# Sliding-window attention and a two-layer MLP in one kernel: the first batch's v by heads, w_in's parts moved forward in the queues, and another split of the last output block

## The chip, the cores and the metric

The kernel runs on one core of a Trainium2 chip. A core has five engines, each with its own in-order queue of instructions: TensorE (PE in the profile; its weight loads are listed apart as PEld), VectorE (DVE), ScalarE (ACT), GpSimd (POOL) and SyncE (SP). DMAs are issued from the queues of SP, ACT and POOL and are carried by sixteen DMA engines that all queues share. The metric is the device time of one execution in microseconds (us), lower is better; the median of three runs before the change is 323.84 us (323.29 to 324.63).

## The reference

Attention over 8 batches, 8 heads, 576 positions and a head size of 64, with a distance bias per head and a causal window of 128; its output, as 4608 tokens of 512 features, goes through two matrices with a hard-swish between them. Inputs and output are float32.

```python
scores = scale * np.matmul(q, k.transpose(0, 1, 3, 2))
bias = slopes[:, None, None] * (-np.abs(rel))[None, :, :]
mask = (rel >= 0) & (rel < window)              # window = 128
scores = np.where(mask, scores + bias[None], -1000000000.0)
attn = softmax(scores)                           # with 1e-09 added to the sum
x = np.matmul(attn, v)                           # -> (4608, 512)
h = x @ w_in                                     # w_in: 512 x 2048
out = (h * np.clip(h + 3.0, 0.0, 6.0) / 6.0) @ w_out   # w_out: 2048 x 512
```

## The kernel before

**Units of work.** Attention goes by pairs of heads: pair g = 4 b + hp is heads 2 hp and 2 hp + 1 of batch b, so there are 32 pairs. A pair's 576 positions are five blocks of 128 (the last half filled). Because of the window, a block of queries sees its own block of keys (the "diagonal", tile scd, lines 285 to 297) and the one before (the "off-diagonal", tile sco, lines 313 to 329). For a pair the steps are: q and k are cast to bf16 (tile pr) and transposed on TensorE (tile tp, line 219 in batch 0, lines 242 and 254 later; from batch 4 on by DMA through tbuf, line 199); the transposed pieces are copied from PSUM to qTb and kTb; scores; exponential on ACT to pd and po; masks on POOL (lines 354, 364, 370); the product with v (tile wide or av, lines 383 and 391), where a column of ones in vbuf gives the sum; on DVE a reciprocal and a product (lines 401 and 402, 412 and 413) to avs; then `back` (line 421) transposes avs to xT, the MLP's input.

In batch 0 the bias and the mask are added on TensorE, by matmuls of the identity with a table (tables_diag, line 266, and tables_off, line 299), which the exponential then takes in one instruction of 1024 columns a tile (lines 348 and 335). From batch 1 on the diagonal goes without a table: `exp_diag` makes two exponentials of 512 columns with a bias (line 351), each followed by a mask on POOL (line 354).

The MLP goes by nine blocks nt of 512 tokens. Of each, sixteen "ups" (moe_up, line 462: four matmuls of 512 columns at line 451, a Relu on ACT at line 470, and a product on DVE at line 471 into gbuf) and sixteen "downs" (moe_down, line 474: four matmuls at line 483; every fourth ends an output block of 128 rows, which is copied to osb and stored).

**Order.** The program's order is written out by hand, and each engine runs its instructions in that order. Attention of one batch is interleaved with the MLP of tokens that are ready: `fill(n)` (line 511) issues the next n units, ups and downs in the order of the strings ORDER (line 501). `first_batch` (line 546) is pairs 0 to 3 and the loading of batch 1; `second_batch` (line 606) is pairs 4 to 7, the first block's ups and the loading of w_out and batch 2; `segment` (line 657) is all the rest.

**Loads.** q and k of batch 0 come as eight runs of 288 KB (load_run, line 90), from SP's and ACT's queues. v of batch 0 comes from SP as five blocks of 128 positions, each for all heads (load_tokens, line 108), in packets of 256 B. q and k of batches 1 and 2 come by load_double (line 96): for four heads (a half dp of the batch) and one of q and k, two DMAs of 288 KB. w_in comes in four parts of 512 columns (load_w_in, line 165) and w_out in four of 512 rows (load_w_out, line 170), cast to bf16 on the way, all from POOL's queue; part i of w_in is first needed by up 4 i. Until w_out arrives, its room holds pd and po of batch 0, and the room of gbuf[1] holds those of batch 1. A one-element memset on POOL (lines 176 and 626) is used to hold back a load into a buffer: the load writes the same element and so waits for POOL to come to it.

**PSUM.** Eight banks: two wide buffers "sc" for scores (and for `wide`), two "h", one "av" and one "o".

The last output block (block 8, rows 384 to 511) is made in lines 485 to 493: after the sixteenth matmul of 512 columns ACT copies columns 0 to 255 and DVE 256 to 511 of the same PSUM tile, and ACT's and SP's queues store one half each.

## Time and profile before

| | |
|---|---|
| median of 3 runs | 323.84 us (323.29 to 324.63) |
| the profiled execution's own time | 324.27 us |
| its span, first to last instruction | 322.6 us |
| granted TensorE clock, mean | 0.999 |
| DMA packets, bytes | 131425, 51.90 MB, 118976 of them under 512 B |
| first transpose of batch 0 starts | 5.56 us |
| values of pair 3 start | 19.95 us |
| first up matmul starts | 21.12 us |
| scores of pair 4 start | 26.05 us |
| values of pair 4 start | 41.33 us |
| first down starts | 51.72 us |
| values of pair 8 start | 64.05 us |
| last matmuls end | 318.8 us |

All later times are from the start of the span of this one profiled execution. A row of the timeline shows start, duration, engine, line, operation, what it writes and reads, and in brackets how long the engine was idle before it and whose work or DMA ended that wait. A row of the table by stretches shows the stretch, its length, then each engine's busy time with the number of instructions, the granted clock, the mean busy share of the sixteen DMA engines (packets overlap, so it can exceed 1) and GB/s. Where a text gives the time at which a DMA landed, it is that of the semaphore update in the same trace.

Landings before the change that the steps use: v's blocks of batch 0 at 10.60, 11.76, 13.95, 15.43 and 16.07; w_in's parts, issued at 12.37, 17.82, 27.21 and 27.94, at 20.34, 27.67, 34.33 and 37.73; v of batch 1, last block, at 38.70; w_out's parts, issued at 40.83 to 43.06, at 47.95, 51.65, 54.68 and 58.13; v of batch 2, fourth and fifth block, at 62.56 and 63.53.

### The profile page before, as it was taken

How to read it: one execution, taken by the hardware profiler on the slowest of the kernel's cores; microseconds unless marked ns; L12 is line 12 of the kernel's file. 1: busy time of each engine (PE TensorE's matmuls, PEld its weight loads, DVE VectorE, ACT ScalarE, POOL GpSimd, SP SyncE). 2: the span in 40 equal slices, each digit the busy share in tenths (PEclk: the TensorE clock that was granted, in tenths of full speed). 3: DMA queues.
4: the chain of work that ended last, by engine and by line, in shares of the span. 5: the costliest groups of instructions: out<-in, count | busy, mean ns of one | idle time of the engine just before them, and what ended most of it. 6: DMA issues, size and time to landing. Idle time of an engine off the chain costs nothing.

```text
span 322.6 us, 7017 instructions
## 1 busy us (share of the span) xinstructions
PE 311.8 (97%) x2722; PEld 166.1 (52%) x2722; DVE 173.1 (54%) x338; ACT 195.2 (61%) x334; POOL 140.1 (43%) x249
## 2 busy tenths in 40 slices
PE   7889999999999999999999999999999999999995
PEld 6565465554554454555677654455444444444442
DVE  6767574554356555555555555555556455455500
ACT  4749976877777666766676667666764344244301
POOL 7465592693593767356745665463331000000000
PEclk9999999999999999999999999999999999999999
DMA  7999999999999999999999999932112100000111
GB/s 279 223 323 201 273 243 201 231 232 200 202 255 177 219 214 184 200 223 205 187 191 200 225 190 199 220 84 79 26 50 84 56 34 35 33 33 33 67 65 65
DMA packets 131425, 51.90 MB, mean 161 GB/s; under 512 B 118976, under 2 KB 123328, under 8 KB 131392
## 3 DMA queue, kind: packets, MB, share of 16 engines
q1 hardware_dynamic: 126160, 45.43, 65.7%
q0 software_dynamic: 4224, 4.19, 8.2%
q10 hardware_dynamic: 1008, 1.84, 1.5%
q8 instruction: 21, 0.34, 0.4%
q14 instruction: 12, 0.10, 0.1%
HBM read 36.70 MB, written 9.44 MB: 143 GB/s over the span
## 4 chain that ended last, share of the span: by engine, by line
PE 82%; DMA 7%; ACT 4%; DVE 2%; POOL 2%; issue 1%; POOLq 0%
PE ops L483 37%; PE hps L451 33%; DMA ldbuf<-in_q_dram 3%; PE scd L296 3%; DMA qTb<-tbuf 2%; DMA w_in_sb<-in_moe_w_in_dram 2%; PE av L391 2%; PE av L383 2%; ACT r L470 2%; PE sco L328 1%; PE w L153 1%; ACT kTb L244 1%; DVE kTb L220 1%; PE tp L219 1%; POOL tbuf L194 1%
## 5 line engine op out<-in xcount | busy, mean ns | idle before, releaser
L471 DVE SCALAR_TENSOR_TENSOR gbuf<-r,hps 128x512 bf16<-128x512 f32 x144 | 98.7, 687 | 103.1 <-ACT r L470 101.6
L470 ACT ACTIVATE r<-hps,bias 128x512 f32<-128x512 f32 x144 | 99.0, 689 | 90.1 <-PE hps L451 89.7
L451 PE MATMUL hps<-xT,w_in_sb 128*128 128x512 bf16 (+1 forms) x640 | 144.9, 358 | 1.3 <-DMA w_in_sb<-in_moe_w_in_dram 0.4
L483 PE MATMUL ops<-w_out_sb,gbuf 128*128 128x512 bf16 x576 | 141.3, 379 | 0.0
L451 PEld LDWEIGHTS <-w_in_sb 128*128 128x128 bf16 x640 | 58.9, 98 | 54.7 <-DMA w_in_sb<-in_moe_w_in_dram 1.4
L483 PEld LDWEIGHTS <-gbuf 128*128 128x128 bf16 x576 | 53.8, 98 | 59.1
L354 POOL TENSOR_SCALAR_AFFINE_SELECT pd<-pd 128x512 bf16<-128x512 bf16 x48 | 29.5, 631 | 34.6 <-ACT pd L351 34.6
L364 POOL TENSOR_SCALAR_AFFINE_SELECT po<-po 128x512 bf16<-128x512 bf16 x48 | 30.1, 632 | 32.2 <-ACT po L361 32.1
L351 ACT ACTIVATE pd<-scd,bias_d 128x512 bf16<-128x512 f32 x48 | 31.5, 684 | 5.0 <-PE scd L296 3.6
L194 POOL CAST tbuf<-ldbuf 128x512 bf16<-128x512 f32 (+1 forms) x45 | 25.5, 611 | 18.7 <-DMA qTb<-tbuf 10.4
L498 DVE COPY osb<-ops 128x512 f32<-128x512 f32 x33 | 22.7, 687 | 20.3 <-PE ops L483 20.3
L361 ACT ACTIVATE po<-sco,bias_o 128x512 bf16<-128x512 f32 x48 | 33.0, 688 | 0.0
L402 DVE TENSOR_TENSOR avs<-av,rc 128x384 bf16<-128x384 f32 (+1 forms) x48 | 23.6, 491 | 1.6
L391 PEld LDWEIGHTS <-pd 128*128 128x128 bf16 x192 | 14.4, 97 | 8.3 <-POOL tbuf L194 0.5
L383 PE MATMUL av<-vbuf,po 128*128 128x65 bf16 x192 | 18.1, 193 | 0.5 <-POOL po L364 0.5
L391 PE MATMUL av<-vbuf,pd 128*128 128x65 bf16 x192 | 17.6, 194 | 0.3 <-ACT kTb L244 0.3
L187 POOL CAST vbuf<-ldbuf 128x1024 bf16<-128x1024 f32 x14 | 14.3, 1041 | 4.5 <-DMA ldbuf<-in_v_dram 4.5
L383 PEld LDWEIGHTS <-po 128*128 128x128 bf16 x192 | 14.4, 98 | 3.7 <-POOL po L364 0.7
L367 ACT ACTIVATE p4buf<-sco,bias_d 128x64 bf16<-128x64 f32 x48 | 15.5, 323 | 0.0
L227 POOL CAST pr<-ldbuf 128x576 bf16<-128x576 f32 x20 | 12.8, 667 | 4.1 <-DMA ldbuf<-in_q_dram 2.1
L296 PE MATMUL scd<-qTb,kTb 64*128 64x128 bf16 x256 | 12.7, 219 | 1.7 <-DVE kTb L220 0.9
L296 PEld LDWEIGHTS <-kTb 64*128 64x128 bf16 x256 | 7.2, 94 | 13.4 <-issue 9.7
(94 smaller groups left out, 208.9 us busy)
## 6 DMA issues: line engine op xcount, KB each, us to landing
out_dram<-osb SPq DMA_DIRECT2D x33, 256.0 KB, 2.4
ldbuf<-in_v_dram SPq DMA_DIRECT2D x32, 256.0 KB, 5.5
ldbuf<-in_q_dram SPq DMA_DIRECT2D x20, 256.0 KB, 4.8
ldbuf<-in_k_dram SPq DMA_DIRECT2D x16, 256.0 KB, 4.6
ldbuf<-in_q_dram SPq DMA_DIRECT2D x12, 288.0 KB, 7.2
ldbuf<-in_k_dram SPq DMA_DIRECT2D x12, 288.0 KB, 7.0
w_in_sb<-in_moe_w_in_dram POOLq DMA_DIRECT2D x4, 512.0 KB, 8.9
w_out_sb<-in_moe_w_out_dram POOLq DMA_DIRECT2D x4, 512.0 KB, 11.2
```

The costliest lines, as they stand in the source:

```text
L194: nc.gpsimd.tensor_copy(out=tbuf[:m, :, j, :], in_=s[:m, j, :, :].rearrange("p (i e) d -> p i (e d)", e=2))
L296: nc.tensor.matmul(scd[:, e, ts(j, 128)], lhsT=kT[r, j, :], rhs=qT[r, j, :], start=first, stop=first or j == 3)
L351: nc.scalar.activation(out=pd[:, e, :, :].rearrange("p j c -> p (j c)"), in_=sc[:, e, :], func=ACT.Exp, bias=bias_d[:, h:h + 1], scale=scale)
L354: nc.gpsimd.affine_select(out=pd[:, e, :, :], in_=pd[:, e, :, :], pattern=[[0, 4], [1, 128]], channel_multiplier=-1, base=0, compare_op=AL ...
L361: nc.scalar.activation(out=po[:, e, :, :].rearrange("p j c -> p (j c)"), in_=sc[:, e, :], func=ACT.Exp, bias=bias_o[:, h:h + 1], scale=scale)
L364: nc.gpsimd.affine_select(out=po[:, e, :, :], in_=po[:, e, :, :], pattern=[[0, 4], [-1, 128]], channel_multiplier=1, base=-1, compare_op=A ...
L383: nc.tensor.matmul(out_av, lhsT=po[:, e, qt % 4, :], rhs=vb[:, qt - 1, h, :], start=True, stop=False)
L391: nc.tensor.matmul(out_av, lhsT=d, rhs=vb[:, qt, h, :], start=(qt == 0), stop=True)
L451: nc.tensor.matmul(hps[:, lo:hi], lhsT=w_in_sb[:, ks, ts(ms, 128)], rhs=xT[:, ks, ds(src, hi - lo)], start=(ks == 0), stop=(ks == n_ks - 1))
L470: nc.scalar.activation(out=r6, in_=hps, func=ACT.Relu, bias=bias3[:, 0:1], scale=1.0 / 6.0)
L471: nc.vector.scalar_tensor_tensor(out=gts[nt][:, ms, :], in0=r6, scalar=1.0, in1=hps, op0=ALU.min, op1=ALU.mult)
L483: nc.tensor.matmul(ops[nt, sub], lhsT=gts[nt][:, ms, ts(sub, 128)], rhs=w_out_sb[:, ms, :], start=(ms == 0), stop=(ms == n_ms - 1))
```

## The change

Three things are changed, and the order around them.

1. v of batch 0 is loaded by heads: first the half-filled last block for all heads, then eight loads, each the four full blocks of one head (128 KB, packets of 256 B as before). It is cast by pairs of heads, all on POOL. The values of pairs 0 and 1 are computed between the scores of later pairs, each head in a PSUM bank of its own (`attend_split`). Transposes of q and of k are separate calls with a bank each and are issued a pair earlier; the casts of pairs 2 and 3 go ahead. Ten warm-up matmuls ahead of the first transposes become eight behind them. Pair 3's diagonal goes without a table, as in later batches.
2. On POOL, load_w_in(0) goes ahead of six of the eight heads' casts, load_w_in(1) is issued with two memsets that hold back the loads of batch 1's second half, load_w_in(2) goes ahead of the casts of that half, load_w_in(3) in the midst of them, and a memset behind it holds back v of batch 1. w_out's parts 0 and 1 go behind a k cast of batch 2, parts 2 and 3 behind pair 7's masks and the q cast. The string of block 1's units and the fills in second_batch are arranged anew.
3. The last output block is computed as 384 and 128 columns in two banks: sixteen matmuls and ACT's copy and store for the first, then sixteen, DVE's copy and SP's store for the second.

```diff
+    def load_heads(b):
+        t = tokens(b, "v")
+        nc.sync.dma_start(out=t[:LAST, 4, :, :],
+                          in_=v[b, :, ds(512, LAST), :].rearrange("h p d -> p h d"))
+        for h in range(H):
+            nc.sync.dma_start(out=t[:, 0:4, h, :],
+                              in_=v[b, h, 0:512, :].rearrange("(j p) d -> p j d", p=128))
...
     def second_w_in():
-        nc.gpsimd.memset(w_out_sb[:, 4, 0:1], 0.0)
+        for i in range(2):
+            nc.gpsimd.memset(ldbuf[i][:, 2 * RT * D:2 * RT * D + 1], 0.0)
         load_w_in(1)
...
     def diag_tabled(g):
-        return g < NP
+        return g < NP - 1
...
+    def attend_split(g, tags):
+        avs = st[g, "avs"] = small.tile([128, NQ, 2, D], BF16, tag="avs", name="avs")
+        for e, tag in enumerate(tags):
+            av = BANKS[tag].tile([128, NQ, W], FP32, tag=tag, name="ave",
+                                 padded_shape=[128, NQ, 102])
+            av_matmuls(g, range(NQ), lambda qt, e: av[:, qt, :], (e,))
+            rc = small.tile([128, NQ, 1], FP32, tag="rcs", name="rcs")
+            nc.vector.reciprocal(rc, av[:, :, D:W])
+            nc.vector.tensor_tensor(out=avs[:, :, e, :], in0=av[:, :, 0:D],
+                                    in1=rc.to_broadcast([128, NQ, D]), op=ALU.mult)
...
+    def last_rows(nt, sub, cut=384):
+        rows = ds(nt * NT + sub * 128, 128)
+        osb = opool.tile([128, d_model], FP32, tag="osb", name="osb")
+        for lo, hi, tag, copy, eng in ((0, cut, "o", nc.scalar.copy, nc.scalar),
+                                       (cut, d_model, "h", nc.vector.tensor_copy, nc.sync)):
+            ps = BANKS[tag].tile([128, hi - lo], FP32, tag=tag, name="ops",
+                                 padded_shape=[128, d_model])
+            for ms in range(n_ms):
+                nc.tensor.matmul(ps, lhsT=gts[nt][:, ms, ts(sub, 128)],
+                                 rhs=w_out_sb[:, ms, lo:hi],
+                                 start=(ms == 0), stop=(ms == n_ms - 1))
+            copy(out=osb[:, lo:hi], in_=ps)
+            eng.dma_start(out=out[rows, lo:hi], in_=osb[:, lo:hi])
...
-    ORDER = [("UUDUDUUDUD", "UUDUDUDUD", "UDUDUDD", "UUDDDD"),
+    ORDER = [("UUDUUDUUDUUD", "UDUDUDUD", "UDUDUDD", "UDDDD"),
...
     def first_batch():
-        prepare(0, (V, A))
+        prepare(0, "qk", (V, A))
         warm_up(20)
         tables_diag(0)
         tables_off(0)
-        warm_up(10)
-        transposes(0, (V, A))
+        transposes(0, "q", "h", V)
+        transposes(0, "k", "h", A)
+        prepare(1, "qk", (P, V))
+        warm_up(8)
         scores_diag(0)
-        prepare(1, (P, V))
-        transposes(1, (V, V))
+        transposes(1, "q", "o", V)
+        transposes(1, "k", "av", V)
         scores_off(0)
         exp_full(0)
+        prepare(2, "qk", (P, V))
+        prepare(3, "qk", (P, V))
+        cast_tail(0, P)
+        cast_pair(0, 0, P)
+        load_w_in(0)
+        for hp in range(1, NP):
+            cast_pair(0, hp, P)
+        for nm in "kq":
+            load_double(1, 0, nm, nc.sync)
         scores_diag(1)
...
+        attend_split(0, ("h", "h"))
         scores_off(2)
-        exp_full(2)
+        exp_off_full(2)
         scores_diag(3)
+        exp_diag(3, 0)
+        exp_diag(3, 1)
+        attend_split(1, ("av", "h"))
+        tables_off(3)
         scores_off(3)
-        exp_full(3)
-        cast_v(0, 0, V)
-        cast_v(0, 1, P)
-        load_w_in(0)
-        cast_v(0, 2, V)
-        cast_v(0, 3, V)
-        cast_v(0, 4, P)
-        for dp in range(2):
-            for nm in "kq":
-                load_double(1, dp, nm, nc.sync)
-        load_tokens(1, "v")
-        attend(0)
-        attend(1)
+        exp_off_full(3)
         back(0)
         attend(2)
         back(1)
+        attend(3)
         prepare_double(1, 0, (P, P), early=second_w_in)
-        attend(3)
+        for nm in "kq":
+            load_double(1, 1, nm, nc.sync)
         back(2)
         up_begin(0, 0, 3)
         back(3)
-        wide_double(1, 0, "q", V)
-        prepare_double(1, 1, (P, P))
         load_w_in(2)
+        prepare_double(1, 1, (P,), "k")
         load_w_in(3)
+        nc.gpsimd.memset(ldbuf[3][:, 0:1], 0.0)
+        prepare_double(1, 1, (P,), "q")
+        tokens(1, "v")
+        load_tokens(1, "v")
         for dp in range(2):
             for nm in "kq":
                 load_double(2, dp, nm, nc.sync)
         up_begin(0, 1, 3)
         done[0] = NP
         fill(1)
-        wide_double(1, 0, "k", A)
+        wide_double(1, 0, "k", V)
         fill(2)
+        wide_double(1, 0, "q", A)
+        fill(1)
...
+        prepare_double(2, 0, (P,), "k")
-        for i in range(4):
+        for i in range(2):
             load_w_out(i)
...
-        prepare_double(2, 0, (P, P))
+        prepare_double(2, 0, (P,), "q")
+        load_w_out(2)
+        load_w_out(3)
         nc.gpsimd.memset(ldbuf[2][:, 0:1], 0.0)
         load_tokens(2, "v")
...
-        fill(1)
-        attend(NP)
+        attend_split(NP, ("av", "o"))
```

The second batch's fills, and the place of its transposes of the second half: the fills of pairs 4, 5 and 6 were 2 and 1, 2 and 1, 1 and 2; they become 1 and 2, 2 and 2, 1 and 1. The wide transposes of k and q of the second half stood ahead of the scores of pairs 4 and 5; they now stand ahead of and behind those of pair 5.

## Prediction

> **What bounds the kernel now.** I read the page first, then TensorE's rows in order of time, then the DMA share by stretches, last the rows at the end. The page (engine sums, then 40 slices):
>
> ```profile
> PE 311.8 (97%) x2722; PEld 166.1 (52%) x2722; DVE 173.1 (54%) x338; ACT 195.2 (61%) x334; POOL 140.1 (43%) x249
> PEclk9999999999999999999999999999999999999999
> DMA  7999999999999999999999999932112100000111
> ```
>
> TensorE (PE) is busy for 97%, its granted clock is full, and nothing here takes work off it but two table matmuls. So only its 10.8 us without work can be won: the rows of idle time in front of an instruction sum to 7.0 us, and 3.8 us follow its last matmul. The DMA row is the second bound: saturated from the second slice to the 25th. These rows of TensorE (start, duration, and in brackets the idle time before it and its releaser) hold most of what can go:
>
> ```profile
> 7.05 0.40 PE L296 MATMUL scd<-qTb,kTb 64*128 64x128 bf16 x8 [0.74 <-ACT kTb L220]
> 9.37 0.40 PE L296 MATMUL scd<-qTb,kTb 64*128 64x128 bf16 x8 [0.21 <-DVE kTb L220]
> 12.23 0.40 PE L296 MATMUL scd<-qTb,kTb 64*128 64x128 bf16 x8 [0.37 <-DVE kTb L220]
> 15.10 0.40 PE L296 MATMUL scd<-qTb,kTb 64*128 64x128 bf16 x8 [0.37 <-DVE kTb L220]
> 22.01 0.38 PE L451 MATMUL hps<-xT,w_in_sb 128*128 128x512 bf16 x1 [0.29 <-ACT xT L438]
> 27.72 1.04 PE L451 MATMUL hps<-xT,w_in_sb 128*128 128x512 bf16 x4 [0.31 <-DVE gbuf L471]
> 34.38 1.04 PE L451 MATMUL hps<-xT,w_in_sb 128*128 128x512 bf16 x4 [0.45 <-DMA w_in_sb<-in_moe_w_in_dram]
> ```
>
> Two are DMA waits: 34.38 by name, and 27.72, where w_in's part 1 lands at 27.67, the moment at which DVE's row ends too. Then batch 2, where TensorE shows no wait but has little slack. POOL's cast of v (first row) waits for its DMA and ends at 63.74; TensorE multiplies by it from 64.05:
>
> ```profile
> 62.70 1.04 POOL L187 CAST vbuf<-ldbuf 128x1024 bf16<-128x1024 f32 x1 [0.74 <-DMA ldbuf<-in_v_dram]
> 64.05 0.23 PE L391 MATMUL av<-vbuf,pd 128*128 128x65 bf16 x2
> ```
>
> That slack of 0.3 us decides most of this forecast: whoever moves TensorE ahead by more meets that v.
>
> **Step 1, batch 0 up to pair 3's values: 2.0 us earlier.** (a) Ten warm-ups lie at 4.91 to 5.56 ahead of the first transposes, though DVE's cast of q ends at 5.19. They go behind the transposes, as eight, into the 0.74 us gap: the transposes begin at 5.22, 0.34 us earlier. (b) DVE and TensorE wait for each other here (DVE's copies at 10.75 and 13.62 follow 1.44 and 0.88 us of idleness). With transposes issued a pair ahead into banks "o" and "av", DVE runs on: from 6.4, casts of k 1 to 3 at 0.65 to 0.74 us and copies of pairs 1 to 3 at a pitch of 0.68 us (7.89 to 8.57), six of them, with a short wait for k 3's landing at 9.67: the last copy ends at 13.2, before at 15.0. v's three DVE casts (0.42 us each) move to POOL at 0.61 us. (c) ACT then paces: exponentials of 1.02 us, pair 3's diagonal as two of 0.63 us in place of one of 1.02 (+0.24), the last ending at 17.0 where it was 17.5. Two table matmuls of 512 columns go (0.43 us of TensorE); POOL gets two masks of 0.62 us, in its queue behind v's casts and ahead of batch 1's. (d) attend_split does 18 value matmuls as two nines between the scores; its halves have no row. A half holds 5 reciprocals and 320 products; two of them cost at least the whole (0.22 + 0.82 us, rows of L412 and L413) and at most twice that. I take 1.3 us; they lie on DVE, free after 13.2, beside ACT's work. Then follow back(0), attend(2), back(1), paced by ACT's copies (0.64 us) and TensorE's transposes. Sum: pair 3's values begin at 17.9, before at 19.95.
>
> **Step 2, w_in part 0.** Its first use would move from 21.12 to 18.9, but it lands at 20.34. POOL issues it after q 3's cast, v's last block and heads 0 and 1: at 12.0, before at 12.37. No row shows a load of one head (512 packets of 256 B). Nearest are v's blocks: one of 256 KB lands 1.2 to 2.2 us after the one ahead of it, the last, of 128 KB, 0.64 us after. So I cost nine loads like five, and part 0 lands at 19.9; if undisturbed at 19.0, if heads 0 and 1 come late at 20.8. The DMA page of the Trainium skill ("DMA: Bandwidth & Descriptors", Bandwidth) speaks against small transfers: batch to 1 MiB or more. By it nine loads lose against five; the 0.64 us above says that half the bytes took half the time while the queue was full.
>
> **Step 3, parts 1 to 3.** Part 1 follows the first k cast of batch 1, which now stands on POOL behind pair 3's masks: issued at 18.65, before at 17.82. But the loads of batch 1's second half (four of 288 KB, 0.75 us each at landing intervals) wait for the two memsets issued with it, where before all eight were ahead of it. Both sets, 3.0 us and about 3.3 us (the step between landings of w_out's parts is 3.0 to 3.7), run side by side after 21: I take 26.5 for part 1, ends 25 and 28. Its first user, up 4, is ready at 25.9, so it starts at 26.5 instead of 27.72, with 0.6 us of transposes (L254) left for later: gain 0.6. Parts 2 and 3 are issued at about 22 and 26.5 rather than both at 27.21; part 2 would land near 31, before 34.33, so the 0.45 us stall goes. Pair 4's values, at 41.33 before, would start near 40; the gain is then 1.1 to 1.5 us. What is late next is batch 1's v, now behind part 3: cast at 39.7 before, and the same set of transfers stands ahead of it. That fits by 0.3 us.
>
> **Step 4, the wall at batch 2.** All that is loaded before batch 2's v is the same set in both kernels, and DMA runs without a break from 2 us to 58 us. So v of batch 2 comes earlier only by what DMA wastes now. The DMA share by stretches (the last two columns are share and GB/s):
>
> ```profile
> 12.00:14.00 2.00, 1.77 (x57) 1.35 (x58) 1.12 (x3) 1.42 (x2) 1.25 (x2) 1.00 1.16 179
> 14.00:16.00 2.00, 1.63 (x24) 0.69 (x20) 2.00 (x5) 1.49 (x2) 0.00 (x0) 1.00 0.99 224
> 26.00:28.00 2.00, 1.69 (x17) 0.70 (x15) 1.61 (x3) 2.00 (x5) 1.41 (x3) 1.00 1.09 233
> 28.00:30.00 2.00, 2.00 (x21) 1.06 (x20) 2.00 (x3) 1.78 (x4) 1.92 (x3) 1.00 0.93 172
> 58.00:60.00 2.00, 2.00 (x11) 0.90 (x10) 1.13 (x2) 2.00 (x6) 0.78 (x2) 1.00 0.66 146
> 60.00:62.00 2.00, 2.00 (x29) 1.06 (x27) 1.54 (x3) 1.56 (x4) 1.86 (x3) 1.00 0.86 231
> ```
>
> Stretches with 256 B packets reach 1.2. Against that the first four lack 0.63 x 2 us / 1.2 = 1.05 us, the last two 1.5 us. The change touches the first four: v's half-filled last block goes first, under the k and q loads, and batch 1's v no longer runs alone at 27 to 30. It leaves the bubble at 58 to 62, where SP issues v's fourth block only at 58.2. A new hole of about 0.3 us opens near 21. So v of batch 2 comes 0.75 us earlier; ends 2.3 us earlier (all waste gone) and 1.5 us later (no waste gone, and the later issues below cost DMA time). Gain kept at 64 us: 0.3 + 0.7 = 1.0 us.
>
> w_out is the cover here: parts 0 and 1 go behind two k casts of batch 2, parts 2 and 3 behind pair 7's masks, issued at about 46.2 instead of 42.33. Part 3 landed at 58.13 for a use at 58.57. The new order puts two more ups (0.87 us each) ahead of that use, so it stays near 58.5 with TensorE 1.5 us ahead: cost nothing, with 0.2 us to spare. After 64 us TensorE has only short waits (the longest 0.35 us at 108) and SP's issues follow its pace, so what is kept there is kept.
>
> **Step 5, the end: 0.55 us.** ACT and DVE copy one half each, one after the other, and SP issues last:
>
> ```profile
> 318.85 0.37 ACT L489 COPY osb<-ops 128x256 f32<-128x256 f32 x1 [2.87 <-PE ops L483]
> 319.25 0.42 DVE L490 COPY osb<-ops 128x256 f32<-128x256 f32 x1 [6.62 <-ACT osb L489]
> 319.70 0.33 SPq L492 DMA_DIRECT2D out_dram<-osb  x1
> ```
>
> Now the first 384 columns are complete while the sixteen 128-column matmuls (0.055 us each, the pace of the ten warm-ups, 0.88 us) still run; ACT's copy (between 0.37 and 0.58, say 0.48) hides under them, and DVE copies 128 columns in 0.29 us (by the slope from 0.42 for 256 to 0.69 for 512). SP issues 0.34 us after the last matmul, before 0.88. Bounds: 0.2 (the two copies still serialize) and 0.7 (the smaller store lands sooner too). The additional weight loads cost nothing by the 65-column value matmuls, each with its own 128x128 weights, at a pitch of 0.03 us (16.67, 16.70, 16.73). The Trainium skill, "TensorE: Matmul & The Clock Gate", Back-to-back issue gap, speaks against it: it gives about 81 ns for each 128-column matmul with its weight load. As an estimate from that page the part would take 1.3 us and the end would win only 0.1 us.
>
> **Sum.** 1.0 + 0.55 = 1.55 us off the profiled execution's 324.27 us (span 322.6) is 322.7. The median of the runs is 0.43 us below the profiled one, so on its scale 323.84 - 1.55 = 322.3 us.
>
> **Rivals.** (A) The front's gain passes whole: part 1 in time for 25.9 and v of batch 2 with 1.5 us or more to spare. Then 1.85 us at pair 4's values (39.5 against 41.33) and more with the bubble at 58 gone: 2.4 to 3.2 us, about 321.2. For it: 2.5 us of DMA waste exist. Against: half of them at a place that the change doesn't touch. (B) Nothing but the end: v of batch 2 as late as now gives 0.3 + 0.55, parts of w_in late again less: 323.2. For it: the same bytes stand ahead. (C) Slower: POOL's queue becomes a chain. Batch 1's v waits for a memset behind part 3, which waits for two k casts, which wait for loads that wait for a memset behind another cast; then k of batch 2, then w_out, then v of batch 2. Every us that this chain comes late reaches 64.05. It decides from 0.85 us (0.3 + 0.55); at 3 us late, 66.7 at that place, the time is 323.84 + 3.0 - 0.85 = 326.0. For it: each link is a real wait; against: DMA has other work at each of them.
>
> **Chances.** Forecast 0.38 (gain 0.9 to 2.3), A 0.29, B 0.16, C 0.17. 0.5%, about what a measurement of this kernel can tell from no change, is 1.6 us: the forecast falls 0.22 beyond and 0.16 within it, A beyond, B within, C 0.14 slower and 0.03 within. Faster 0.51, same 0.35, slower 0.14. From 320.6 (nearly all of A) to 325.4 (C up to 2.4 us late) 8 in 10 should lie.
>
> **What would show it.** Pair 3's values near 18 us and the first up matmul held by w_in until 19.9 (steps 1 and 2); up 4 near 26.5 with a wait for w_in (3); batch 2's first value matmul waiting for POOL's cast of v, near 63 (4): without that wait A, with it at 64 or later B or C; SP's last issue 0.34 us behind the last matmul (5). It is wrong from the root if DMA's order, not its total, sets when v of batch 2 lands.

## The result and the profile after

The kernel after takes 327.66 us (median of 6 runs, 327.48 to 328.93), the one before 324.08 us on the same chip (6 runs, 323.29 to 325.86): ratio 1.0101, 95% interval 1.0080 to 1.0122. It is slower, by more than the prediction's range allowed. The profiled execution took 327.62 us, its span is 325.9. The page's lines that answer to those of before:

```profile
PE 313.1 (96%) x2734; PEld 167.9 (52%) x2734; DVE 173.3 (53%) x342; ACT 195.5 (60%) x335; POOL 142.5 (44%) x255
...
PEclk9999999999999999999999999999999999999999
DMA  7989999999999999999899999942011200000111
```

The DMA row has 8s where it had 9s. TensorE's busy time grew by 1.3 us and its idle time by 2.0 us. Of the 1.3 us, 0.7 lie between 4.5 and 7.5 us (3.00 us busy against 2.26) and are no added work: in this execution the full clock was granted from 7.46 us on, in that of before from 4.56, and 36 transposes took 1.17 us at 5.38 but 0.75 us at 7.77. That late start costs nothing further on: the run e10 below, with the full clock from 4.24 on, comes to the first row here at the same 13.70. TensorE's rows in order of time:

```profile
13.70 0.38 PE L308 MATMUL scd<-qTb,kTb 64*128 64x128 bf16 x7 [0.59 <-issue]
...
19.22 0.44 PE L455 MATMUL tb<-ident,avs 128*128 128x128 bf16 x5 [0.72 <-ACT xT L461]
19.49 0.23 PE L403 MATMUL wide<-vbuf,w_out_sb 128*128 128x65 bf16 x2
...
28.68 0.39 PE L474 MATMUL hps<-xT,w_in_sb 128*128 128x512 bf16 x1 [1.32 <-DMA w_in_sb<-in_moe_w_in_dram]
...
66.80 0.23 PE L403 MATMUL av<-vbuf,pd 128*128 128x65 bf16 x2
...
67.67 0.19 PE L403 MATMUL av<-vbuf,pd 128*128 128x65 bf16 x1 [0.49 <-POOL vbuf L199]
```

The row of before that answers to the last one:

```profile
64.27 0.19 PE L391 MATMUL av<-vbuf,pd 128*128 128x65 bf16 x1
```

Pair 3's values start at 19.49 (before 19.95), the first up at 20.85 (21.12): batch 0 is a little earlier. Up 4 (28.68, before 27.72) waits 1.32 us for w_in's part 1; pair 4's values start at 42.90 (41.33). Batch 2's first value matmuls start at 66.80 (64.05). The eighth of them is the first to read v's second cast; it now waits for POOL until 67.67, where before it started at 64.27 without a wait: 3.40 us late. The last matmul ends 3.72 us later (322.53 against 318.81). So nearly all of the loss is there by batch 2.

Where it starts, in POOL's rows. First before, then after:

```profile
16.76 0.67 POOL L227 CAST pr<-ldbuf 128x576 bf16<-128x576 f32 x1
17.78 0.10 POOL L176 MEMSET w_out_sb<- 128x1 bf16 x1 [0.35 <-PE wide L391]
17.82 0.74 POOL L166 DMA_DIRECT2D w_in_sb<-in_moe_w_in_dram  x1
```

```profile
17.49 0.63 POOL L192 CAST vbuf<-ldbuf 128x512 bf16<-128x512 f32 x1 [2.15 <-DMA ldbuf<-in_v_dram]
18.07 1.22 POOL L366 TENSOR_SCALAR_AFFINE_SELECT w_out_sb<-w_out_sb 128x512 bf16<-128x512 bf16 x2
20.71 0.66 POOL L241 CAST pr<-ldbuf 128x576 bf16<-128x576 f32 x1 [1.42 <-DMA ldbuf<-in_k_dram]
21.31 0.14 POOL L185 MEMSET ldbuf<- 128x1 f32 x2
21.39 0.76 POOL L174 DMA_DIRECT2D w_in_sb<-in_moe_w_in_dram  x1
```

POOL first waits 2.15 us for head 7, the last of v's loads (landed 17.44), so that pair 3's masks end at 19.29. Then the first cast of batch 1's k waits 1.42 us for its own load, which landed at 20.56 (before 16.61). Behind the cast stand the memsets that hold the second half's loads, and w_in's part 1: issued 3.6 us later than before. What that does to the DMA engines shows in the stretches (granted clock, DMA share and GB/s are the last three columns), first before, then after:

```profile
16.00:24.00 8.00, 6.64 (x122) 5.31 (x122) 5.02 (x11) 3.76 (x6) 5.15 (x9) 1.00 1.11 323
24.00:40.00 16.00, 15.25 (x147) 7.88 (x144) 10.49 (x14) 15.02 (x23) 8.32 (x13) 1.00 1.13 233
40.00:64.00 24.00, 23.33 (x248) 13.43 (x247) 14.80 (x26) 18.60 (x31) 15.01 (x25) 1.00 1.08 225
```

```profile
16.00:24.00 8.00, 6.38 (x100) 4.39 (x97) 3.88 (x10) 5.18 (x9) 5.09 (x11) 1.00 0.85 213
24.00:40.00 16.00, 14.27 (x136) 7.60 (x133) 11.22 (x14) 13.67 (x21) 7.58 (x13) 1.00 1.18 240
40.00:64.00 24.00, 22.00 (x231) 12.28 (x225) 13.51 (x25) 18.47 (x30) 14.63 (x25) 1.00 1.07 228
```

From 16 to 24 us the DMA engines deliver (323 - 213) x 8 us = 0.88 MB less. Later they win back (240 - 233) x 16 + (228 - 225) x 24 = 0.18 MB. The missing 0.70 MB at 228 GB/s are 3.1 us. Another 0.33 MB were missing at 16 us already (3.74 against 4.07 MB), which makes 4.5 us in all; the fourth block of batch 2's v lands 3.9 us later (66.45 against 62.56). The hole itself, and the four stretches in which the prediction wanted waste to go:

```profile
12.00:14.00 2.00, 1.41 (x36) 0.70 (x30) 1.59 (x3) 0.79 (x1) 1.61 (x3) 1.00 0.87 163
14.00:16.00 2.00, 2.00 (x54) 1.71 (x52) 1.00 (x4) 1.48 (x2) 0.99 (x2) 1.00 0.99 136
20.00:22.00 2.00, 1.51 (x16) 0.72 (x13) 1.04 (x2) 0.97 (x2) 1.29 (x4) 1.00 0.58 213
22.00:24.00 2.00, 1.83 (x20) 1.19 (x19) 0.32 (x1) 0.74 (x2) 2.00 (x5) 1.00 0.57 54
26.00:28.00 2.00, 0.94 (x11) 0.36 (x9) 1.78 (x4) 1.91 (x3) 0.67 (x1) 1.00 1.15 292
28.00:30.00 2.00, 1.32 (x8) 0.66 (x8) 0.40 (x1) 1.08 (x3) 0.98 (x2) 1.00 1.14 298
```

At 12 to 16 less is moved than before (163 and 136 GB/s against 179 and 224), 26 to 30 is better (292 and 298 against 233 and 172), and 20 to 24 is new. The end, last: ACT's copy no longer ends the kernel, and SP issues 0.36 us behind the last matmul (0.89 before).

```profile
321.68 0.48 ACT L508 COPY osb<-ops 128x384 f32<-128x384 f32 x1 [2.01 <-PE ops L505]
...
322.57 0.29 DVE L508 COPY osb<-ops 128x128 f32<-128x128 f32 x1 [6.25 <-PE ops L505]
322.89 0.33 SPq L509 DMA_DIRECT2D out_dram<-osb  x1
```

### The profile page after: what moved, and what is told of

Same layout as the page of the kernel before. It is cut to its first block, busy times and chain, and to the rows that moved or that the text cites. A ratio compares the mean times of both kernels' runs of the same rounds, so it can differ in the third digit from the quotient of the medians.

```text
span 325.9 us, 7055 instructions
## 1 busy us (share of the span) xinstructions
PE 313.1 (96%) x2734; PEld 167.9 (52%) x2734; DVE 173.3 (53%) x342; ACT 195.5 (60%) x335; POOL 142.5 (44%) x255
## 4 chain that ended last, share of the span: by engine, by line
PE 80%; DMA 6%; POOL 4%; SPq 4%; issue 2%; ACT 1%; DVE 1%; POOLq 0%
PE ops L524 36%; PE hps L474 31%; DMA ldbuf<-in_v_dram 4%; SPq L112 4%; PE scd L308 2%; PE av L403 2%; DMA ldbuf<-in_k_dram 2%; PE av L395 2%; PE sco L340 1%; PE ops L505 1%; PE w L161 1%; POOL pr L241 1%; PE tp L232 1%; ACT xT L461 1%; POOL vbuf L199 1%
## 5 line engine op out<-in xcount | busy, mean ns | idle before, releaser
L524 PE MATMUL ops<-w_out_sb,gbuf 128*128 128x512 bf16 x560 | 138.0, 379 | 0.4 <-DMA w_out_sb<-in_moe_w_out_dram 0.3
L524 PEld LDWEIGHTS <-gbuf 128*128 128x128 bf16 x560 | 52.1, 98 | 57.7 <-issue 0.6
L403 PE MATMUL av<-vbuf,pd 128*128 128x65 bf16 x192 | 17.9, 194 | 0.8 <-POOL vbuf L199 0.5
```

The source lines that it names most:

```text
L403: nc.tensor.matmul(out_av, lhsT=d, rhs=vb[:, qt, h, :], start=(qt == 0), stop=True)
L524: nc.tensor.matmul(ops[nt, sub], lhsT=gts[nt][:, ms, ts(sub, 128)], rhs=w_out_sb[:, ms, :], start=(ms == 0), stop=(ms == n_ms - 1))
```

## The experiments

The theory at first (T): the holds leave the DMA engines without work at 20 to 24, and all later loads are late by it. Rivals: batch 0's new order costs by itself; w_out's new place costs (W). Medians and ratios stand against the kernel before on the same chip (324.25 to 324.83 us). Before moved by up to 0.75 us between chips, so small differences between kernels on different chips are read from the ratios. A profile is one execution and can lie 1 to 3 us from the median.

The granted clock has to be read beside the times. In all executions of the change, e1, e2, e3 and e9 its mean was 0.998 or more. In other kernels some executions had less (0.988 to 0.995 in e10 and e11), and most of these are 1 to 3 us longer than the rest of the same kernel; where the argument needs it, the text says so.

**The end alone** (e1_tail_only): the kernel before with `last_rows`.

> The kernel before with the last output block as 384 and 128 columns and nothing else. In the changed kernel 3.36 us lie between the end of the last matmul and the end of the span, before 3.8. Theory T (the loss is all in the loading chain of the first 65 us): this part alone gives 0.3 to 0.6 us less than before, about 323.5. Rival (the split of the last block costs as much as it wins, as two groups of matmuls, two banks): within 0.2 us of before, or slower.

323.69 us, ratio 0.9979 (0.9959 to 0.9999): 0.77 us faster. The end's gain is real, though the interval only just leaves out no change, and what precedes it in the change loses 3.58 + 0.77 = 4.35 us by the medians, 4.0 by the ratios.

**Without the first hold** (e2_no_hold): all eight loads of batch 1's k and q ahead of POOL's cast.

```diff
-        for i in range(2):
-            nc.gpsimd.memset(ldbuf[i][:, 2 * RT * D:2 * RT * D + 1], 0.0)
...
-        for nm in "kq":
-            load_double(1, 0, nm, nc.sync)
+        for dp in range(2):
+            for nm in "kq":
+                load_double(1, dp, nm, nc.sync)
```

> The changed kernel, in which the second half of batch 1's q and k is issued right behind the first half and no memset holds it back; w_in's part 1 still follows the first k cast. Theory T (the two memsets behind a cast that waits for k's landing at 20.6 stop SP's queue, DMA runs dry at 21 to 23, and all that follows comes late by that): the hole closes, v of batch 2 lands 1.5 to 2.5 us earlier than 66.45, the time is 325.0 to 326.2, and the wait for w_in part 1 (1.3 us) may stay or grow, since these loads then stand ahead of it. Rival R (loading v by heads is what costs): no change, 327.4 or more.

325.01 us, 1.0026 (1.0007 to 1.0045): 2.65 us of the loss gone by the medians (2.4 by the ratios), as T said. In all ten executions the clock was 0.998 or more. 16 to 24 us delivers as much as before or more, and v of batch 2 no longer holds TensorE:

```profile
16.00:24.00 8.00, 6.40 (x94) 4.35 (x90) 3.71 (x11) 5.30 (x10) 5.67 (x9) 1.00 1.10 350
```

**w_in's part 1 ahead of the cast** (e3_w1_early, the memsets with it), and **both** (e5_both).

```diff
-        prepare_double(1, 0, (P, P), early=second_w_in)
+        second_w_in()
+        prepare_double(1, 0, (P, P))
```

> The changed kernel, in which the two memsets and w_in's part 1 go ahead of the first k cast of batch 1 on POOL instead of behind it, so that they no longer wait for k's landing: issued at 19.4 instead of 21.4. Theory T: all links of the chain come 1.5 to 2 us earlier, the wait for part 1 (1.3 us) goes, pair 8's values start near 65.5 instead of 67.7; time 325.3 to 326.2. Rival R: no change but the wait for part 1, whose 1.3 us come back as a wait for v of batch 2: 327.4.

> The changed kernel without the hold on the second half of batch 1's q and k, and with w_in's part 1 ahead of the first k cast on POOL (the edits of the two runs before together). Theory T (one chain, cut at two places): part 1 lands before 27, its wait goes, and DMA has no hole near 21; the time is 324.0 to 325.0, no better than the sum of the two gains allows, since v of batch 2 lands at about 62.5 to 63 by DMA's total. If the two edits were about different losses, their gains (2.6 and 1.9 us) would add up to 323.2.

e3: 325.79 us, 1.0048 (1.0033 to 1.0063), as T said, again with 0.998 or more in all ten. e5: 325.77 us, 1.0037 (1.0014 to 1.0060). The two edits don't add up, and T's 324 to 325 for e5 is missed by 0.8: with all loads early, part 1 stands among the second half's loads and lands at 28.5, with a wait of 1.16 us.

**v by blocks of positions** (e4_v_blocks): `load_heads(0)` replaced by `load_tokens(0, "v")`.

> The changed kernel with v of batch 0 loaded in five blocks for all heads as before, and cast by pairs of heads as in the change (each cast then needs all five blocks, so pairs 0 and 1 come later). Rival R (nine loads by head are what costs, the last lands at 17.44 where the last block landed at 16.07, and k of batch 1 is issued 1.2 us later): 1 us or more faster, 326.5 or less. Theory T: the start of the chain (k's landing at 20.6) moves by at most 1 us, w_in's part 0 is issued 3 to 4 us later as it stands behind the casts of pair 0; the time gets longer, 327.7 to 330.

328.64 us, 1.0133 (1.0110 to 1.0156): loading v as before does not bring the time back. It does not clear the loading by heads either. Against T, k's landing moved by 3.8 us, to 16.77 (k was issued at 12.25, with part 0 behind it at 17.40), so how v is loaded does bear on when k lands. What e4 loses, it loses elsewhere: all four executions had a clock of 0.989 to 0.995, and pair 0's values need all blocks and wait:

```profile
17.51 0.19 PE L403 MATMUL ave<-vbuf,w_out_sb 128*128 128x65 bf16 x1 [3.18 <-POOL vbuf L192]
```

**The holds on the kernel before** (e6_hold_on_before): the memsets, the second half and v of batch 1 behind the first k cast.

> The kernel before with the hold alone: two memsets behind the first k cast, together with w_in's part 1 as in the change; the loads of batch 1's second half and its v follow behind them on SP. Theory T (the hold costs by what it waits for): before, k lands at 16.6 and the cast ends at 17.4, so the loads are issued at 17.6 while DMA still has work until 21.5: within 0.6 us of before, 323.5 to 324.8. Rival H (holding these loads back costs as such, since fewer transfers are queued): 1.5 us or more slower than before, as in the changed kernel, 325.5 to 326.5.

325.57 us, 1.0038 (1.0012 to 1.0063): by the time inside H's interval, but only 1.1 us slower than before on the same chip, where H asked for 1.5 or more. The holds cost there too, but less where k lands early (17.41 in its profile).

**w_out's place** (e7_w_out_back: e5 with w_out's loads, batch 2's casts and ORDER of before; e12_no_w_out_23: the change without the loads of w_out's rows 1024 to 2047, so their products are not the reference's).

> As e5_both, and in addition w_out's four parts and batch 2's casts at their places of before, with the old string of block 1's units. Theory T (w_out and v of batch 2 stand in one queue that the front has already made late, and the two casts ahead of w_out wait for loads that have landed by then): within 0.6 us of e5_both. Rival W (the part of the loss that e2 left, 1 us against before, is w_out behind the casts): 0.7 us or more faster than e5_both.

> The changed kernel that leaves out the loads of w_out's parts 2 and 3 (rows 1024 to 2047; what then stands in their room is used instead): 6.6 us less for DMA ahead of batch 2's v, and nothing else changed. Theory T (what makes batch 2 late is that v lands behind all other transfers): pair 8's values no longer wait; D 3 neither; of the 3.6 us by which the first values of pair 8 are late against before, 1.5 to 2.5 go, and the time is 325.2 to 326.2. Rival (all of the lateness is made before 53 us, where the first down stands 1.6 us late, and by TensorE's own waits): 327 or more.

e7: 324.97 us, 1.0017 (0.9995 to 1.0038), 0.8 us less than e5: slightly for W. e12: 325.08 us, 1.0023 (0.9994 to 1.0053), 2.6 us less than the change. Without those two loads v of batch 2 lands in time, and pair 8's values start at 65.87 with no wait: the wall at batch 2 carries most of the loss to the end.

**Pair 3's transposes later** (e8_swap3: e5 with them behind pair 2's diagonal scores).

> As e5_both, with pair 3's transposes behind pair 2's diagonal scores instead of ahead of them. In the changed kernel pair 2's scores stand still from 12.9 to 13.7, until DVE's copy of pair 3's k ends at 13.6, though pair 2's copies end at 12.24. If the order is what makes them wait, the scores run at 12.4, ACT's exponential of pair 2 starts 1 us earlier, and pair 3's values begin at 18.3 to 18.8 instead of 19.5; the total time gains at most 0.3 us by theory T, since v of batch 2 decides; by the rival that the front of TensorE decides it gains 0.8 us or more.

325.33 us, 1.0031 (1.0010 to 1.0052), no difference to e5. The wait near 13.7 stays and only changes its instruction; more on it at the end.

```profile
13.69 0.28 PE L230 MATMUL tp<-ident,pr 64*64 64x64 bf16 x7 [0.71 <-issue]
```

**The end, and w_in's parts 2 and 3 earlier, on before** (e9_tail_w23): both loads called ahead of `prepare_double(1, 1, (P, P))`.

> The kernel before with two parts of the change alone: the last block as 384 and 128 columns, and w_in's parts 2 and 3 issued ahead of the casts of batch 1's second half. Theory T (parts 2 and 3 then wait for no cast, and DMA has the same total): part 2 lands 2 us or more earlier, its wait (0.45 us in the profile of before) goes, batch 1's v lands as late as before or later by less than the slack there; with the end's 0.45 to 0.75 us the time is 323.0 to 323.6, below before. Rival (whatever goes ahead pushes batch 1's v back, and with it w_out and batch 2's v): 324.3 or more.

324.06 us, 0.9977 (0.9955 to 0.9999): faster than before, between T and the rival by its median, and nothing tells it from e1. The wait for part 2 goes, one of 0.75 us for w_out's part 3 comes.

**Batch 0's new order and the end, with the loads of before** (e10_part_1_3), and **the change without both holds** (e11_no_holds: the second half and v of batch 1 issued right behind the first half).

> Parts 1 and 3 of the change with all loads of batch 1, w_in and w_out in the order of before: batch 0's v by heads, its values between the scores, the new fills up to pair 7, and the split of the last block, but no holds, w_in 1 behind the first k cast, parts 2 and 3 behind the casts of the second half, batch 1's v issued with q and k, w_out in one group, the old string of units. Theory T (the whole loss is the queue order of part 2, and part 1's gain meets DMA's total at batch 2): 323.2 to 324.2. Rival F (batch 0's new order costs by itself, through v's later landing, 17.4 against 16.1, and TensorE's wait at 13.4 to 13.7): 324.8 or more.

> The changed kernel without either hold: the second half of batch 1's q and k and batch 1's v are issued right behind the first half; all POOL orders stay as in the change. Theory T (each hold lets DMA run dry once, at 21 to 23 and at 39 to 44): batch 1's v lands by 38, earlier than the 38.4 of the run without the first hold, and w_in 1 and 2 later, as v stands ahead of them: their waits grow by 1 us or more; v of batch 2 no later than 62.9; time 324.5 to 325.5. Rival (the hold of v is what kept the rest late): 324.0 or less.

327.12 us, 1.0063 (1.0036 to 1.0089), and 327.79 us, 1.0086 (1.0054 to 1.0117). By these medians **T falls here**: the DMA engines are full (354 and 345 GB/s at 16 to 24), and the time is nearly the change's. Part 1 is issued at 20.7 and 21.3, behind the same late k, but now with the second half and v of batch 1 ahead of it, and lands at 30. e10:

```profile
29.94 0.39 PE L472 MATMUL hps<-xT,w_in_sb 128*128 128x512 bf16 x1 [2.77 <-DMA w_in_sb<-in_moe_w_in_dram]
```

But the medians mix two kinds of execution. Four of e10's twelve and three of e11's eleven had a clock of 0.999 or more; they took 324.54 to 325.96 us and 325.46 to 326.08 us, about 2 us less than the change, which is about what e2 won. The others, at 0.988 to 0.995, took 326.32 to 330.01 us. In e11's profile (328.36 us) the clock is 0.50 from 30.30 to 33.72, right behind a wait of 2.96 us for part 1. So the holds do cost, as T said. What T left out is that the released loads then stand ahead of part 1, and that the longer wait for it can cost the clock too. Even at full clock e10 stays above T's 324.2, in three of four executions in F's range: batch 0's new order costs by itself.

**Part 1 untied, with the loads of before** (e15_p13_w1_early: e10 with e3's edit).

> Like e10_part_1_3, but w_in's part 1 called ahead of batch 1's first k cast on POOL, so that it hangs on no load at all. Theory: issued near 18.5, lands near 28, a wait of at most 0.7 us, 324.3 to 325.5; with the end's 0.8 us in it that leaves batch 0's new order at a loss of 0 to 1 us. Rival (the new order of batch 0 costs in another way): 326.5 or more; a gain of the front that passes whole would be 323.2 or less.

325.45 us, 1.0036 (1.0006 to 1.0066): inside T's interval, 1.7 us below e10 by the medians and 0.9 by the ratios, whose intervals overlap. Most of that is the clock: eight of its eleven executions had 0.999 or more, and they took 324.77 to 325.62 us, hardly less than e10's four. The mechanism isn't shown: the profile is one of the other three, and there POOL waited for head 7 (landed 20.32), so that part 1 was issued only at 22.13 instead of 18.5. By both readings e15 is 1.8 us behind e1: batch 0's new order, without holds and with part 1 tied to no load of its own, costs about that much.

**The late k itself.** New theory (K): k's landing at 20.6 is the root. e13_k_first, e14_p13_k_first, e16_k_first_own and e17_p13_k_first_own issue k's first half ahead of heads 6 and 7.

```diff
         for h in range(H):
+            if h == 6:
+                load_half(1, 0, "k", 0, nc.sync)
```

> The change with one transfer moved: the first k half of batch 1 is issued on SP ahead of heads 6 and 7 of v of batch 0, instead of behind all nine and behind w_in's part 0. Theory (the late landing of that k is the root: the memsets, w_in's part 1 and the held loads all hang on its cast): it lands by 17.5 instead of 20.6, POOL casts it when its own queue lets it, near 18.5, the memsets and w_in's part 1 follow near 19.2, the DMA share at 20 to 24 is above 0.9 (0.56 in the change), v of batch 1 and of batch 2 come 2 us earlier, and the time is 325.0 to 326.2, about what calling w_in 1 ahead of the cast gave. Rival (heads 6 and 7, 0.8 us later, hold POOL's last cast of v and pair 3's values, and nothing is won): 327 or more.

> Batch 0's new order and the new end, with the loads of before (e10_part_1_3), and the same one transfer moved ahead of heads 6 and 7. Theory (e10's loss came from w_in's part 1 issued 3 us late, behind the second half and v of batch 1): part 1 is issued by 19.3 instead of 20.7, the wait of 2.8 us for it falls to 1.3 or less, 324.5 to 325.7. Rival (the new order of batch 0 costs in another way, not by that load): the wait goes and the time stays at 326.5 or more.

> The idea of e14 without its fault (the k half in a buffer of its own): batch 0's new order and the new end, the loads of before, k's first half ahead of heads 6 and 7. Theory: w_in's part 1 issued by 20 instead of 20.7, the wait of 2.8 us for it down to 1.5 or less, 324.5 to 325.9 (e15, which unties part 1 from that k, gave 325.45). Rival (batch 0's new order costs in another way): the wait goes and the time stays at 326.5 or more.

These three say nothing on K: e13 took 335.21 us (1.0327, 1.0286 to 1.0368), e14 332.52 (1.0240, 1.0200 to 1.0280), e17 336.00 (1.0353, 1.0332 to 1.0375). In e13 and e14 the load shares a buffer with batch 0's k, and being called first, it makes batch 0's cast wait for it and read batch 1's k; in e17 v of batch 1 is called ahead of the cast that reads the same buffer, which so reads v. The waits, e13's:

```profile
15.56 0.37 PE L238 MATMUL tp<-ident,pr 64*64 64x64 bf16 x6 [9.49 <-ACT pr L226]
```

> The idea of e13 without its fault: there the k half went into the buffer in which the k of batch 0's pair 0 lay, and batch 0's first cast waited for it, 9.5 us (its pair 0 was computed from batch 1's k). Here the half goes into the end of the buffer of batch 1's v, which is empty until then. Theory (that k's late landing is the root): it lands by 17 instead of 20.6, cast near 18.5 to 19.3, memsets and w_in's part 1 at 19.2 to 20, DMA share at 20 to 24 above 0.9, v of batch 1 and 2 earlier by 1.5 to 2.5 us, 325.0 to 326.2. Rival (heads 6 and 7 come 0.8 us later, hold POOL's last cast of v and pair 3's values, and eat the gain): 327 or more.

e16, with the load in a free place: 327.76 us, 1.0140 (1.0098 to 1.0181), as slow as the change, also in its one execution at 0.998 (327.76; the other four had 0.990 to 0.995). In its profile (330.86 us, 3 above its median, so that the effect may be smaller in the others) k lands at 15.5, but head 7 has taken its place behind w_in's part 0 (issued at 12.41, landed at 20.22), and POOL's queue waits for that head ahead of k's cast:

```profile
20.34 0.62 POOL L203 CAST vbuf<-ldbuf 128x512 bf16<-128x512 f32 x1 [4.94 <-DMA ldbuf<-in_v_dram]
20.92 1.22 POOL L377 TENSOR_SCALAR_AFFINE_SELECT w_out_sb<-w_out_sb 128x512 bf16<-128x512 bf16 x2
22.09 0.65 POOL L252 CAST pr<-ldbuf 128x576 bf16<-128x576 f32 x1
```

**Part 0 behind both** (e18_w0_later): `load_w_in(0)` behind the cast of heads 2 and 3.

> The change with one call moved: w_in's part 0 is issued by POOL behind the cast of heads 2 and 3 instead of heads 0 and 1, near 14.4 us instead of 12.5, so that it no longer starts ahead of the last head of v and of batch 1's first k (issued at 12.6 and 13.3). In every run so far a transfer that SP issued 0.35 us or more behind w_in's part 0 landed at 19.6 to 20.9, and one issued ahead of it by 16.8. Theory (that order is the root): head 7 lands by 16.5, k's first half by 18 instead of 20.6, POOL's first k cast starts behind its masks at 19.3 instead of 20.7, the memsets and w_in's part 1 follow at 20.0, the DMA share at 20 to 24 rises from 0.56 to 0.8 or more; w_in's part 0 lands near 21, so that the first up matmul is up to 0.5 us later. Together 325.8 to 326.9. Rival (the order against part 0 does not matter, the nine loads simply take their time): k lands at 20 or later all the same, 327.3 or more.

328.07 us, 1.0118 (1.0087 to 1.0150). The mechanism came as said: head 7 lands at 15.9, k at 16.7, and the cast no longer waits. The time did not: part 0 lands at 22.6, and TensorE waits for it. Part 1, issued 2.0 us earlier than in the change, lands 1.9 us later (30.49 against 28.63), and TensorE waits again.

```profile
18.68 0.65 POOL L241 CAST pr<-ldbuf 128x576 bf16<-128x576 f32 x1
19.28 0.13 POOL L185 MEMSET ldbuf<- 128x1 f32 x2
19.35 0.76 POOL L174 DMA_DIRECT2D w_in_sb<-in_moe_w_in_dram  x1
```

```profile
22.67 0.61 PE L474 MATMUL hps<-xT,w_in_sb 128*128 128x512 bf16 x1 [1.56 <-DMA w_in_sb<-in_moe_w_in_dram]
...
30.54 0.39 PE L474 MATMUL hps<-xT,w_in_sb 128*128 128x512 bf16 x1 [0.67 <-DMA w_in_sb<-in_moe_w_in_dram]
```

```profile
16.00:24.00 8.00, 5.31 (x89) 3.65 (x88) 3.79 (x10) 4.72 (x7) 5.98 (x12) 0.89 1.01 218
```

The share is 1.01 where the change had 0.85, and yet it delivers 218 GB/s, as little as the change's 213. The released second half was issued at 19.44 to 21.33, all behind part 1 (19.35), and lands only at 27.7 to 32.2. In before its loads went ahead of part 1 and landed 0.8 to 1.6 us apart, by 26.5. A hole in the share is thus not needed for the loss: what counts, by these runs, is which loads stand behind one of w_in's. The second wait also hides what the first one and the low clock behind it (0.50 from 22.3 to 25.7) cost in this execution.

**What follows.** Three orders of the same three transfers (head 7, k, part 0) give 327.66, 327.76 and 328.07 us: whichever is last is paid for. That the three are so near each other is in part chance, since all six executions of the change had the full clock and all six of e18 had 0.988 to 0.995. The order is near a tie: in the profiles of after, e11, e15 and e16 head 7 is issued 0.14 to 0.40 us behind part 0, in those of e2, e3 and e10 0.9 us or more ahead of it. The two edits that recover 2 us or so each take a load out of a chain, either the second half (e2) or part 1 (e3). Shown, at full clock: the first hold costs about 2.5 us (e2), part 1's tie to the late k 1.7 to 1.9 us (e3), both less when the other is there no more (e5); w_out's place, up to 0.8 us, is within the measurements' width. K alone is refuted: an early k gains nothing when another of the three is late for it. Not settled: what the 1.8 us of e15 against e1 consists of, and in which executions TensorE's clock falls.

The versions that beat the kernel before are e1 and e9, both with no more than the new end and, in e9, two loads moved.

## Why the prediction was wrong, by its own steps

**Step 1** (pair 3's values at 17.9; came 19.49). The row at 13.70 put a floor under the front: TensorE stood still until then with no releaser in the profile (why is argued in the last section), and ACT's next exponential followed at 14.11 after 1.32 us of idleness. back(1) waited 0.72 us for ACT's copy, which was not in the sum. Of the 2.0 us 0.46 came.

**Step 2** (part 0 at 19.9; came 20.45, inside its ends). "I cost nine loads like five" held for part 0 and failed for what stands behind: SP was done issuing the nine at 13.15 instead of 11.97, so k was issued at 13.27, 0.8 us behind part 0 instead of 0.3 us ahead of it. I had not asked who changes places.

**Step 3 is where it failed**: "issued at 18.65" assumed that k's load is there when POOL gets to it, and that POOL gets to it near 18. POOL came at 19.29, having waited for head 7, and k at 20.56; of the 2.74 us by which part 1 was issued late (21.39), 1.42 are the wait for k. "0.75 us each" for the held loads is the step of loads that land alone; beside part 1 the same four had landed 1.3 to 1.6 us apart in before (22.21 to 26.54) and did so again (1.4 to 2.8 us). "Both sets run side by side" was read as 26.5; part 1 landed at 28.63, outside my 25 to 28, and up 4 was 1.0 us later instead of 1.2 us earlier. Parts 2 and 3 were issued at 23.98 and 29.63, not 22 and 26.5.

**Step 4**: "All that is loaded before batch 2's v is the same set" is true and was the wrong measure. By the packets, 14.78 MB had started by 60 us before and 13.85 MB after. The hole of 0.3 us expected near 21 became, against a share of 1.11 (before, 16 to 24), (1.11 - 0.575) x 4 / 1.11 = 1.9 us. "That fits by 0.3 us" for batch 1's v: it was issued behind a memset at 30.36 and landed at 41.70 (38.70), w_out's last part at 63.01 instead of 58.5. "That slack of 0.3 us" was misread: the cast that ends at 63.74 is first read at 64.27, so the slack was 0.5. The prediction's last sentence named the case: DMA's order, not its total, sets when v of batch 2 lands.

**Step 5** held: both copies took what was estimated (0.48 and 0.29 us), the span's end lies 0.40 us nearer to the last matmul (0.55 predicted), e1 gives 0.77 by the medians and 0.68 by the ratio.

**Rival C** was the mechanism, with the links in the order it gave, though it did not name the late k at the head of the chain; it priced 3 us late at 326.0. TensorE's last matmul came 3.72 us late, 3.40 of it by batch 2's values, and C's 0.85 us of credit was too much, since the slack is already in that lateness and the end gave 0.40: 324.08 + 3.72 - 0.40 = 327.4, measured 327.66. It had 0.17. What spoke against it ("DMA has other work at each of them") was the error: the first link left the engines with 54 GB/s.

## What to carry to other kernels

When a load is split into more issues, write down, per queue, who now stands behind the next big transfer of another queue, and which cast that late one gates; here 1.2 us of issuing became 3.6 us of lateness. Before a load is tied to a computation, check that the computation's own input cannot be the load that comes last. Read GB/s beside the share: full engines can deliver little (e18 at 16 to 24 us: a share of 1.01 and 218 GB/s; e10: 1.10 and 354). And read each execution's clock beside its time before a median decides between two theories.

## What the runs showed of the hardware

- **Behind a cast load, a transfer waits.** In the 16 kernels that issue w_in's part 0 at 11.8 to 12.6 us, the first transfer that SP issued 0.35 us or more behind it landed between 0.7 us ahead of and 2.3 us behind that part (e10: part 0 issued 12.22, landed 18.47; k issued 13.00, landed 19.95). What was issued at most 0.23 us behind it landed 1.3 us or more ahead, by 18.1. In e4 and e18, which issue part 0 at 17.40 and 14.67, the loads that SP issued at 13.07 to 13.75 landed by 18.98 without it; in the change the one issued at 13.27 landed at 20.56. The Trainium skill, "DMA: Bandwidth & Descriptors", Queues, rings and completion order, has each DMA engine take packets from its queues in turn, by which, as I read it, k would have moved along with part 0. These landings look more like one line, though they don't show where it forms.
- **TensorE stands at one fixed place of its instructions.** In the fourteen traced kernels with the new front (e13 and e14, held up earlier, aside) TensorE stands 0.4 to 1.4 us until 13.4 to 14.0, with no releaser, and each time at its 448th record (matmuls and weight loads counted together). e8 put another instruction there, and the wait stayed. In before that record was issued near 13.5 with no wait, so the old front may just not have been fast enough to meet it. The first packet of 16 KB on the queue of kind "instruction" starts at 10.25 in before and at 10.89 in after and takes 1.3 us, no more than some later ones (0.9 to 1.4 us). That TensorE waits for instructions is argued, not shown.
- **The clock falls after short waits, not after each.** In e18 it was 0.50 from 22.3 to 25.7, behind a wait of 1.56 us:

```profile
22.00:23.00 1.00, 0.33 (x1) 0.13 (x2) 0.00 (x0) 0.00 (x0) 0.83 (x2) 0.64 0.94 166
23.00:25.00 2.00, 2.00 (x10) 1.10 (x9) 0.00 (x0) 0.30 (x1) 0.00 (x0) 0.50 1.00 211
25.00:26.00 1.00, 1.00 (x6) 0.34 (x4) 0.32 (x1) 0.07 (x1) 0.00 (x0) 0.65 0.99 192
```

The matmul at 22.67 took 0.61 us, at 28.68 in the change 0.39. e11 lost it from 30.30 to 33.72 behind a wait of 2.96 us, while e10's profile kept 1.00 behind one of 2.77; eight of e10's twelve executions, of one and the same program, had a mean of 0.988 to 0.995. The Trainium skill, "TensorE: Matmul & The Clock Gate", What's actually happening, gives a free-running activity window of about 3.4 us, and the 3.4 us for which the low clock lasts agree with that. Such a window could make one wait cost the clock and the next one not, which no run here shows. That a whole idle window is needed, as the page's table has it, is not borne out by a wait of 1.56 us.
